# Writing phase products from SBUF into operand tiles, and weaving the first mixing visit between the phase steps

## The chip, the cores and the metric

One core of one Trainium2 chip. The metric is device time of one execution in microseconds (us). Executions of one kernel in one set spread over 0.1 to 0.6 %, so only differences whose intervals lie apart are taken as shown. A run of the kernel before always lies beside a run of a variant, on the same chip. Two variants that were not run in the same call are compared through the kernel before, and such a difference is uncertain by some 6 to 9 us where the intervals are widest (both taken together). Engines are named as the profile names them: PE (TensorE matmul), PEld (its weight load), DVE (VectorE), ACT (ScalarE), POOL (GpSimd), SP (SyncE).

## The reference, cut to what matters

```python
def reference(x, h, w_theta, w_tok_r, w_tok_i, w_ch):   # x: (8, 5696, 128), h: (5696, 128)
    y = causal_convolution_by_fft(x, h)                  # (8, 5696, 128)
    theta = y @ w_theta
    zr, zi = y * cos(theta), y * sin(theta)              # "phase products"
    mix = w_tok_r @ zr + w_tok_i @ zi                    # over 5696 tokens, for each batch: "mixing"
    u = y + mix
    return u + maximum(u @ w_ch, 0)
```

The mixing is most of the work: two 5696 x 5696 weights against 1024 columns (8 batches of 128). The kernel splits 5632 = 2 x 2816 of the tokens in both directions and forms the 2 x 2 block product with seven products instead of four (Strassen-Winograd style), which needs sums of operand blocks.

## The kernel before: the parts that the change touches

Three stages matter. The FFT leaves y (transposed) in memory and partly in SBUF. The **phase steps** turn 22 token tiles of 128, in two halves of four batches, into zr and zi. The **mixing visits** follow: the first full one of each of two passes (one for each half of the input tokens) is "classic" (four products, 176 matmuls of 512 columns), while the other full ones use seven products and the operand sums.

A phase step: four PE transposes, ten matmuls for theta, one DVE copy out of PSUM, three ACT functions, two DVE products, then stores:

```python
def phase_step(ti, hh):                       # tile ti, half hh of the batches
    ps = psum()
    ...                                       # transposes into tpz, then:
    y_ap = st["sby"].tile([P, 4, D], BF16, tag="y", name="y_ap")     # slots: 2 in half 0, 4 in half 1
    def copy():
        nc.vector.tensor_copy(y_ap, tpz)
        nc.sync.dma_start(y2_hbm[ti]..., y_ap...)                   # y is needed again later
    phases_b(ti, y_ap, ..., copy=copy)

def phases_b(...):
    ...                                       # theta matmuls
    if copy is not None: copy()
    nc.scalar.activation(mag, r, AF.Abs)
    nc.scalar.activation(red, r, AF.Sin, ...)
    nc.scalar.activation(mag, mag, AF.Sin, ...)
    zz = fh.tile(...)
    zi_eng.tensor_mul(zi, red, yflat)         # DVE
    nc.vector.tensor_mul(zr, mag, yflat)
    ...
    nc.sync.dma_start(z_hbm[:, p_, j, i, :, cols].rearrange("z t n -> t z n"), zz[rows])
```

So every product goes to memory (`z_hbm`) and comes back as one of eleven operand tiles `b` (1 MB each). The steps of both halves run first, then the visits:

```python
for n, ti in enumerate(tile_order):           # 22 steps of the second half
    phase_step(ti, 1)
    ...                                       # every fourth: load finished operand tiles
...                                           # pools of the mixing are opened only here
for i, (k, p, tt, j0, s0, nj) in enumerate(stretches):   # 3 operand tiles a stretch
    if (p, tt, j0 + s0) in ((1, None, 0), (1, 1, 0)):    # DVE in written order: start of pass 2 only
        ...
    if classic:                               # first visit of a pass
        for n in range(4):
            for j in range(nj): ... four matmuls
            aside(n == 0, n == 2)             # a "background" phase step of a later tile
        for j in range(nj):
            sums_apart(...); sums_in_place(...)   # five DVE sums for each operand tile
```

## Time and profile before

| | us |
|---|---|
| median of the runs | 2174.2 |
| first second-half copy on DVE | 477.9 |
| first mixing matmul | 549.4 |
| second visit begins | 590.8 |
| PE full from about | 596 |

I add one table: columns are the stretch and its length, then busy us (number of instructions) of PE, PEld, DVE, ACT and POOL, then PE's granted clock, the share of the DMA engines and GB/s. The kernel before, by stages:

```profile
478.00:500.00 22.00, 13.99 (x147) 10.14 (x149) 18.39 (x34) 17.80 (x32) 0.00 (x0) 0.96 0.87 224
500.00:520.00 20.00, 10.59 (x86) 8.07 (x88) 15.06 (x28) 11.63 (x21) 7.54 (x17) 0.67 1.01 255
520.00:540.00 20.00, 4.71 (x41) 3.18 (x38) 11.85 (x23) 7.75 (x14) 6.01 (x12) 0.67 1.13 291
540.00:560.00 20.00, 10.40 (x37) 4.41 (x39) 10.55 (x21) 2.74 (x5) 10.51 (x20) 0.63 1.15 287
560.00:580.00 20.00, 19.89 (x101) 9.43 (x102) 17.12 (x31) 4.33 (x7) 6.12 (x12) 1.00 1.04 266
580.00:600.00 20.00, 17.69 (x79) 7.88 (x80) 17.54 (x32) 3.73 (x6) 3.77 (x8) 0.91 0.72 158
600.00:640.00 40.00, 39.79 (x204) 19.01 (x206) 31.69 (x62) 12.38 (x20) 16.54 (x31) 1.00 0.79 153
```

Read PE downwards: 14, 11, 5, 10, then 20 of 20. From 500 to 560 no engine is full, while the DMA share is above 1.0 of its nominal: the steps and the read-back of their products wait on transfers. That hole is what the change is after.

### The profile page before, as it was taken

Reading aid. Unit: us, or ns where it says so; the run is one execution under the profiler, and the core shown is the slowest. Engines: PE = TensorE matmul, PEld = TensorE weight load, DVE = VectorE, ACT = ScalarE, POOL = GpSimd, SP = SyncE. Lnnn points to the kernel's source line nnn. Section 1 sums busy time; section 2 is a strip of 40 time slices with the busy share of each in tenths; the row PEclk is TensorE's granted clock in tenths of the full one; section 3 lists DMA queues with packets and bytes.
Section 4 is the critical chain, followed back from the end, with each engine's and each line's share of the span. In section 5 each row is a group of like instructions: output and inputs, shape, how many; then the busy total and the mean of one; then the engine's idle time right before and its main releaser. Section 6 shows DMA issues by size and latency. Waiting matters only on the chain.

```text
span 2175.5 us, 41105 instructions
## 1 busy us (share of the span) xinstructions
PE 1998.2 (92%) x15545; PEld 1125.1 (52%) x15723; DVE 1619.4 (74%) x2920; ACT 670.6 (31%) x984; POOL 857.1 (39%) x1572
## 2 busy tenths in 40 slices
PE   4788898763899999999999999899999999999998
PEld 4787888652344444444444444344444444444444
DVE  7767767767778888888877667667777777776867
ACT  5877877574132333333210000001111111111111
POOL 5301010002344645445466544354545453535350
PEclk8788889987899999999999999999999999999999
DMA  7356463579988989899999869687878787879794
GB/s 146 89 125 163 128 162 118 172 185 275 236 156 175 182 169 168 167 179 176 176 169 162 138 115 291 106 133 137 148 132 152 132 151 130 152 131 153 126 158 91
DMA packets 409382, 340.38 MB, mean 156 GB/s; under 512 B 83303, under 2 KB 363751, under 8 KB 408071
## 3 DMA queue, kind: packets, MB, share of 16 engines
q0 software_dynamic: 221312, 143.00, 48.7%
q1 hardware_dynamic: 183552, 179.93, 28.5%
q10 hardware_dynamic: 4320, 14.81, 1.8%
q8 instruction: 123, 2.02, 0.4%
q14 instruction: 75, 0.61, 0.1%
HBM read 381.83 MB, written 97.93 MB: 221 GB/s over the span
## 4 chain that ended last, share of the span: by engine, by line
PE 65%; DMA 5%; DVE 4%; issue 2%; ACT 2%; POOL 1%; SPq 1%; DVEq 0%; ACTq 0%; POOLq 0%
PE m L910 59%; DMA b<-z_hbm 3%; PE m L878 2%; DMA z_hbm<-zz 2%; DVE c L917 1%; PE v L680 1%; PE utp L673 1%; PE m L914 1%; DVE wt L591 1%; PE m L833 1%; POOL wb L582 1%; PE m L831 1%; ACT mag L404 0%; ACT red L405 0%; PE theta_ps L382 0%
## 5 line engine op out<-in xcount | busy, mean ns | idle before, releaser
L582 POOL DMA_DIRECT2D wb<-in_moe_w_tok_i_dram x720 | 387.9, 547 | 679.3 <-DVE wt L591 602.6
L591 DVE STREAM_TRANSPOSE wt<-wb 128x384 f32<-128x384 f32 (+2 forms) x720 | 360.2, 524 | 117.1 <-PE m L910 71.2
L582 POOL DMA_DIRECT2D wb<-in_moe_w_tok_r_dram x720 | 386.6, 548 | 146.2 <-DVE wt L591 107.0
L910 PE MATMUL m<-b,wt 128*128 128x512 bf16 x1803 | 425.7, 381 | 7.1 <-DVE wt L591 2.4
L910 PEld LDWEIGHTS <-wt 128*128 128x128 bf16 x1848 | 181.3, 98 | 225.0 <-issue 5.7
L917 DVE TENSOR_TENSOR c<-c,m 128x512 f32<-128x512 f32 x420 | 271.0, 671 | 0.4 <-PE m L910 0.4
L675 ACT ACTIVATE uts<-utp 128x512 bf16<-128x512 bf16 (+1 forms) x90 | 53.2, 592 | 607.3 <-PE utp L673 607.3
L320 PE MATMUL ps<-r_u,u_t 128*128 128x128 f16 x1024 | 133.0, 228 | 14.9 <-DVE u_t L304 11.7
L321 PE MATMUL ps<-r_v,v_t 128*128 128x128 f16 x1024 | 131.7, 227 | 0.0
L670 ACT ACTIVATE ub<-c 128x512 bf16<-128x512 f32 (+1 forms) x90 | 56.3, 628 | 224.9 <-DVE c L846 139.7
L127 POOL DMA_DIRECT2D x<-in_x_dram x64 | 34.2, 541 | 201.3 <-PE ps L190 189.3
L320 PEld LDWEIGHTS <-u_t 128*128 128x128 f16 x1024 | 106.0, 103 | 13.6 <-DVE u_t L304 13.5
L321 PEld LDWEIGHTS <-v_t 128*128 128x128 f16 x1024 | 104.9, 103 | 5.2 <-issue 3.7
L304 DVE TENSOR_TENSOR u_t<-xs,hs 128x1024 f16<-128x1024 f16 x96 | 69.6, 725 | 41.9 <-ACT xs L302 31.5
L302 ACT ACTIVATE xs<-ps 128x1024 f16<-128x1024 f32 x96 | 95.3, 1017 | 17.6 <-DVE v_t L304 8.7
L878 PE MATMUL m<-b,wt 128*128 128x512 bf16 x344 | 79.3, 387 | 15.3 <-ACT red L405 14.5
L190 PE MATMUL ps<-f_t,x 89*128 89x180 f16 x512 | 84.5, 310 | 8.0 <-ACT xs L302 5.9
L208 PEld LDWEIGHTS <-w_t 64*128 64x128 f16 x3240 | 65.5, 106 | 38.1 <-issue 24.7
L580 POOL COPY wb<-b 128x2 bf16<-128x2 bf16 x4 | 0.5, 179 | 213.2 <-DMA z_hbm<-zz 213.2
L190 PEld LDWEIGHTS <-x 89*128 89x128 f16 x512 | 73.8, 237 | 10.1 <-issue 9.4
L384 ACT ACTIVATE red<-theta_ps,magic 128x512 f32<-128x512 f32 (+1 forms) x46 | 31.6, 687 | 140.8 <-PE theta_ps L382 107.4
L623 ACT ACTIVATE yb<-tpz 128x512 bf16<-128x512 bf16 (+1 forms) x46 | 27.4, 597 | 153.6 <-PE tpz L621 137.4
(2713 smaller groups left out, 3824.5 us busy)
## 6 DMA issues: line engine op xcount, KB each, us to landing
wb<-in_moe_w_tok_r_dram POOLq DMA_DIRECT2D x352, 96.0 KB, 4.5
wb<-in_moe_w_tok_i_dram POOLq DMA_DIRECT2D x352, 96.0 KB, 5.0
wb<-in_moe_w_tok_r_dram POOLq DMA_DIRECT2D x352, 80.0 KB, 4.2
wb<-in_moe_w_tok_i_dram POOLq DMA_DIRECT2D x352, 80.0 KB, 3.7
hs<-hf_hbm SPq DMA_DIRECT2D x192, 128.0 KB, 3.2
cp_hbm<-c SPq DMA_DIRECT2D x88, 256.0 KB, 2.3
c<-cp_hbm SPq DMA_DIRECT2D x88, 256.0 KB, 4.0
out_dram<-c SPq DMA_DIRECT2D x88, 256.0 KB, 4.2
```

The lines of the kernel that those rows point to most:

```text
L190: nc.tensor.matmul(ps[:, i // 2, (i % 2) * 2 * K1:(i % 2 + 1) * 2 * K1], lhs(q + i), f1_t[:NB], start=True, stop=True)
L208: nc.tensor.matmul(ps[:, e, j * HD:(j + 1) * HD], w_t2[rows, c0 + j, N2 * (1 - ri):N2 * (3 - ri)], a_st["a"][rows, ri * K1 + c0 + j, :], s ...
L302: nc.scalar.activation(xs[:, :, :, :ck], ps, AF.Copy)
L304: nc.vector.tensor_tensor(uv[r][:, :, :, c0:c0 + ck], xs[:, :, :, :ck], hv[:, r:r + 1, :, :ck].to_broadcast([P, 2, HD, ck]), op=mult)
L320: nc.tensor.matmul(o, u_t[:, at:at + P], r_u, start=True, stop=False)
L321: nc.tensor.matmul(o, v_t[:, at:at + P], r_v, start=False, stop=True)
L582: nc.gpsimd.dma_start(wb[32 * i:32 * i + 32, :ng, :nj * 64], bass.AP(tensor=a.tensor, offset=a.offset + row0 * S + p * H + i * QR + j0 * 6 ...
L591: nc.vector.transpose(wt.rearrange("p j t r -> p (j t r)").bitcast(F32).rearrange("p (j g t) -> p g j t", j=TJ, g=4)[:, :ng, :nj], wb[:, : ...
L670: nc.scalar.activation(ub[:m].rearrange("p b d -> p (b d)"), c[:m], AF.Copy)
L878: nc.tensor.matmul(ms[n // 2 * 2 + h], a[n][:, j, :, r], bts[jj][n % 2 * 2 + h][:, r, :], start=(n % 2 == 0 and jj == 0 and r == 0), stop= ...
L910: nc.tensor.matmul(ms[q], a[q][:, j, :, r], bts[jj][q][:, r, :], start=(jj == 0 and r == 0), stop=(jj == NJ - 1 and r == 1 and q not in left))
L917: nc.vector.tensor_tensor(c, z, ms[q], op=op)
```

## The change

Its intent: for nine of the eleven operand tiles the second half's products go from SBUF straight into the operand tile (the first half is loaded beforehand), weights can be loaded early into the place of an FFT table, and the first visit's matmuls are woven between the last twelve phase steps. The sums of operands are spread over steps and visit, and DVE is put in written ("program") order from the first of the ten steps that precede the first visit to the third stretch of the second.

```diff
+                for r in range(2):                            # products: SBUF -> operand tile
+                    (nc.gpsimd if e and r else nc.sync).dma_start(
+                        home[j][32 * i:32 * i + 32, :4096]....[:, :, q_, r], zz[e * 64 + r:e * 64 + 64:2])
 ...
+    def load_b_half(j):                                       # first half, from memory, on POOL
+        t_ = home_of[j] = tile_b(0, j, home_pool(j))
+        for z in range(2):
+            nc.gpsimd.dma_start(t_[:, z * 2048:z * 2048 + 1024], z_hbm[z, 0, j, 0]...)
 ...
+            (nc.gpsimd if hh else nc.sync).dma_start(y2_hbm[ti]..., y_ap...)
 ...
-    for n, ti in enumerate(tile_order):
-        phase_step(ti, 1)
+    steps1 = [lambda ti=ti: phase_step(ti, 1) for ti in tile_order]
+    def next_steps(n):
+        if steps1:
+            for _ in range(n):
+                steps1.pop(0)()
+                done["steps"] += 1
+                sum_some(1)                                   # one operand sum that is due
 ...
-            if (p, tt, j0 + s0) in ((1, None, 0), (1, 1, 0)):
-                if tt is None:
+        if (p, tt, j0 + s0) in ((0, 0, 0), (0, 1, 6), (1, None, 0), (1, 1, 0)):
+            if tt != 1:
                 ordered.enter_context(tc.manual_schedule(engines={mybir.EngineType.DVE}))
 ...
+                next_steps(10)                                # ten steps ahead of the first visit
 ...
                 for j in range(nj):
                     ...four matmuls
+                    if p == 0:
+                        if steps1:
+                            next_steps(1)                     # twelve steps woven into its first stretch
+                        else:
+                            sum_some(1)
```

What `manual_schedule` does can be read from the traces: inside it DVE's instructions stand as they are written; outside it the build puts them in an order of its own.

## The prediction

> **What bounds the kernel now.** I read the page's engine rows first, then a table of stages, then the waits and the DVE groups inside the one stage where PE is idle. Page, busy tenths in 40 slices (54 us each):
>
> ```profile
> PE   4788898763899999999999999899999999999998
> ...
> PEclk8788889987899999999999999999999999999999
> DMA  7356463579988989899999869687878787879794
> ```
>
> PE is full from slice 12 on. The hole is in slices 9 to 11 (435 to 600 us), where the granted clock sags too while DMA is at 8 to 9 tenths. The same by stage; columns are busy us (instructions) of PE, PEld, DVE, ACT, POOL, then clock, DMA share, GB/s:
>
> ```profile
> 440.00:478.00 38.00, 24.92 (x323) 19.63 (x330) 21.67 (x39) 26.68 (x45) 0.00 (x0) 0.84 0.77 190
> 478.00:550.00 72.00, 29.88 (x272) 21.75 (x277) 53.92 (x99) 39.92 (x69) 19.59 (x40) 0.74 1.01 260
> 550.00:595.60 45.60, 42.99 (x201) 19.72 (x205) 34.37 (x62) 8.07 (x13) 13.28 (x25) 0.95 0.94 229
> 595.60:1286.00 690.40, 684.01 (x3393) 322.21 (x3462) 554.79 (x1082) 170.50 (x275) 358.58 (x660) 1.00 0.93 166
> 1286.00:1420.00 134.00, 124.75 (x563) 56.92 (x570) 87.45 (x170) 4.80 (x9) 57.05 (x107) 0.96 0.82 185
> 1420.00:2160.00 740.00, 735.89 (x3839) 354.09 (x3915) 546.01 (x1064) 97.16 (x162) 342.19 (x638) 1.00 0.79 139
> ```
>
> From 595.6 on PE is 99% busy, so each us by which that steady state starts earlier is a us off the end. Two stages lie ahead of it and run one after the other: the 22 phase steps on batches 4 to 7 (478 to 550), then the first ("classic") mixing visit with its 176 matmuls (550 to 595.6). Neither fills an engine: in 117.6 us PE is busy 72.9, DVE 88.3, ACT 48.0. Why the first takes 72 us, from the waits in 478 to 550:
>
> ```profile
> POOL wb L580 <- DMA z_hbm<-zz: 213.2, 1, 213.2
> ACT mag L404 <- DVE y_ap L486: 32.1, 13, 9.8
> PE ps L482 <- ACT red L405: 26.9, 14, 10.2
> ...
> PE m L878 <- ACT red L405: 14.5, 1, 14.5
> PEld L878 <- DVE y_ap L486: 13.5, 1, 13.5
> DVE b L543 <- DMA b<-z_hbm: 11.3, 6, 4.6
> ```
>
> The mixing matmul m stands behind the last phase step; the weight loads stand behind phase products that go to memory (z_hbm) and come back; DVE, in order, stands behind the read-back of b, and the phase steps behind DVE. DVE groups of 478 to 596 (count, then busy us and mean ns):
>
> ```profile
> L415 DVE TENSOR_TENSOR zz<-mag,y_ap 128x512 bf16<-128x512 f32 x24 | 16.5, 686 | 0.0
> ...
> L486 DVE COPY y_ap<-ps 128x512 bf16<-128x512 bf16 x22 | 9.2, 419 | 2.4 <-DMA y_hbm<-y_ap 1.9 <-PE ps L399 0.4
> L591 DVE STREAM_TRANSPOSE wt<-wb 128x384 f32<-128x384 f32 x17 | 8.7, 553 | 4.0 <-DMA wb<-in_moe_w_tok_i_dram 4.0
> L543 DVE TENSOR_TENSOR b<-b 128x1024 bf16<-128x1024 bf16 x11 | 7.6, 688 | 16.2 <-DMA b<-z_hbm 16.2
> ```
>
> In the timeline these overlap by some 0.08 us: start to start 0.60 for a product or an operand sum, 0.34 for a copy, 0.50 for a transpose. I use those.
>
> **What the Trainium skill says.** (1) "Perfetto Trace Analysis", section Optimization Strategy: where the busiest engine changes between regimes, interleaving the regimes can help. That is this change, and the table above is the case: ACT and DVE lead in the first stage, PE in the second. (2) "TensorE: Matmul & The Clock Gate", section What's actually happening: PE falls to half clock after about 3.4 us without work and needs about as long to recover. The trace agrees: clock 0.50 in 540 to 550, 0.77 in 550 to 560, 1.00 in 560 to 590, and the steps' wide matmuls start 0.43 us apart after a gap, 0.22 otherwise. (3) "VectorE: DVE Perf Modes", section The perf-mode tier table: a tensor_tensor on bf16 in SBUF reaches 2x and no more, so spreading the 55 sums does not make one cheaper; 1024 columns in 0.60 us at 0.96 GHz is 1.8 a cycle. (4) "DMA: Bandwidth & Descriptors", section Issuing engines are not separate DMA queues: transfers from SP, ACT and POOL share the same 16 engines. So moving stores to POOL buys only issue time; the trace is at a DMA share of 1.01 here.
>
> **The change part by part.** It doesn't change the arithmetic; it moves it.
>
> Products: for 9 of 11 operand tiles the second half of z goes straight from SBUF into the tile. Read-back falls from 9 x 1 MB to 9 x 0.5 MB, so 4.7 MB less of the 21.6 MB moved in 478 to 560: at 263 GB/s 18 us of DMA time, mostly not on the path as such, but it removes DVE's 16.2 us wait for the read-back. Cost: 4 DMAs of 64 KB per step instead of 2 of 128 KB, one on POOL.
>
> Weights: the ring lies where an FFT table was, so its first loads leave when the last FFT stage lets go (about 405 us), no longer behind z. The 213 us POOL wait goes; it cost only the 4 us that a transpose waited.
>
> Weaving, with DVE kept in program order. Ten steps come first; each then stands behind 4 mixing matmuls.
> - Ten steps: DVE 10 x (0.34 + 2 x 0.60) = 15.4, and about 4 sums that are ready, 2.4: 17.8 us. ACT (1.66 a step in the trace): 16.6. DVE sets it.
> - Two sets of weight transposes, 8 x 0.50: 4.0.
> - Twelve woven steps: DVE 12 x (1.54 + 0.60 for a sum) = 25.7; PE 12 x (1.1 + 4 x 0.216) = 23.6; ACT 20. DVE again.
> - The other 128 matmuls: PE 27.6 + 1 for two background steps. DVE 32 sums 19.2, 8 transposes 3.5, two background steps 3.6, four adds 2.4, the next visit's weights 4.4: 33.1. DVE again; some 7 of 55 sums are left for the next visit, whose DVE is 80% busy and takes them.
> Sum 80.6 us, against the 117.6 of now. From 478 the steady state would start at 558.6: 37 us earlier, 38 with the 1.2 us of half clock just after 595.6. So the stage stays bound by DVE and not by PE (63 us).
>
> Then I take off, as estimates: 2.5 us for a later start, since the read-back of the first halves (9 x 0.5 MB) now falls into 440 to 478, where DMA stood at 254 GB/s and share 0.99 in 460 to 470; and 6 us of DVE waits on transfers, because POOL now issues 16 weight loads of 0.547 us (8.8 us) right when the woven steps need it for their y and z pieces, while y has four buffers (about 6.5 us). That leaves 29.5.
>
> Second pass: its classic visit finishes two of four sums earlier, and the in-place operand sums leave the tail (now 5.2 us from 1406.1 to 1411.4): 2 to 3 us gained. Against it, b is read back in 2 KB rather than 4 KB pieces where PE already waits 4.0 us for it: 1 to 2 us lost. Net +1.
>
> 2174.2 - 29.5 - 1 = 2143.7; I say 2145.
>
> **The rivals.**
> - Clean overlap: transfers never stall DVE and the start does not slip. 38 to 40 us gained: 2134 to 2136. More needs a start before 478. For: a DMA share with 18 us less in it. Against: steps now wait up to 10 us on stores, and their number grows.
> - Queues fill: z pieces land as late as now (up to 11.5 us at the worst), DVE in program order waits at a sum, and POOL's loads hold up stores. 15 to 20 us lost again: 2155 to 2165. For: z_hbm stores land after 5.6 us (median) in this stage, a sum is let in two steps (3.4 to 4.3 us) after its last product.
> - Lockstep: today ACT's first operation of a step starts just after that step's copy (the 32.1 us row). If that is a true dependence and DVE stays in program order, the next copy follows this step's products, which follow ACT: about 1.7 + 0.7 + 0.6 + 0.5 = 3.5 us a step, 22 x 3.5 = 77 us for what I count as 43.5. That eats the gain: about 2175. Against: theta and the transposed y now lie in different PSUM tiles, so ACT need not wait for the copy.
>
> **Range and chances.** The first rival bounds it below, the second above; half the lockstep would give 2160. So 2130 to 2165. Faster by over 2% means under 2130.7, 43.5 us off, which is more than DVE's work allows from a start at 478: 0.13. Slower by over 2% (over 2217.7) needs a stall in every later visit: 0.03. Within 2%: 0.84.
>
> **What would show it.** Right: the steady state starts near 566; DVE over 90% busy from the first second-half step to it, PE near 70% at clock 1.00; no DVE wait on the read-back of b; PE after it unchanged at 99%. Wrong: a period near 3.5 us between ACT's Abs operations (lockstep); DVE sums waiting on zz transfers or copies on y stores for over 10 us (queues); the first half of the steps ending well before or after 478; or PE below 98% in the later visits through late weight loads.

## The result, and the profile after

The kernel after took 2178.7 us (median of 4 runs, 2173.95 to 2179.79), the kernel before 2173.25 us (2172.23 to 2176.88) beside it. The ratio is 1.0018 with a 95 % interval of 0.9998 to 1.0037. All ratios here are the mean time of one kernel's runs over the mean of the other's of the same rounds, so not quite the ratio of the medians quoted. Executions over 1.5% slower than the fastest of the same kernel are left out of the means. The predicted 29.5 us did not come. The profiled execution of after is its fastest one (2173.95), and that of before is one of its slower ones (2177.26): in the two profiles after is 3.3 us the shorter, though its median is the longer. So a lead of some 3 us that is left at a point of these two profiles is no gain.

The kernel after, the same stages as above:

```profile
478.00:500.00 22.00, 12.09 (x108) 8.77 (x109) 13.99 (x26) 15.54 (x27) 11.01 (x20) 0.72 0.94 311
500.00:520.00 20.00, 16.55 (x138) 10.06 (x139) 19.37 (x37) 12.55 (x23) 10.41 (x19) 1.00 0.64 137
520.00:540.00 20.00, 19.20 (x134) 10.54 (x134) 12.22 (x23) 9.99 (x18) 11.26 (x21) 1.00 0.79 188
540.00:560.00 20.00, 13.90 (x63) 6.18 (x62) 14.04 (x25) 5.27 (x9) 2.15 (x4) 0.83 0.81 230
560.00:580.00 20.00, 9.26 (x51) 4.51 (x49) 18.30 (x33) 6.42 (x11) 8.64 (x16) 0.90 0.81 147
580.00:600.00 20.00, 16.89 (x70) 7.47 (x73) 13.42 (x27) 0.00 (x0) 8.54 (x16) 0.85 0.66 119
600.00:640.00 40.00, 34.62 (x165) 15.55 (x166) 32.71 (x65) 12.84 (x21) 13.83 (x26) 0.96 0.72 138
```

The hole from 500 to 540 is filled (PE 36 of 40 instead of 15), and the first mixing matmul comes at 508.3 instead of 549.4. But a new hole lies at 540 to 600: PE 40 of 60, where before had 48 of 60, and even 600 to 640 isn't full. The 41 us of lead shrink to 7.8 when the second visit begins (583.0 against 590.8), and to 2.6 at its last add (632.84 against 635.45), which is no more than the two profiled executions differ by. The DMA share is below 0.85 from 500 on, so the DMA engines as a whole are no longer full; single stores are still waited for, as shown below.

DVE isn't full in that hole either, and its timeline shows why (columns: start, duration, engine, line, operation, tiles, forms, count, and in brackets the idle time just before and what ended it). The kernel after, DVE, from the last step on:

```profile
545.59 0.68 DVE L622 TENSOR_TENSOR b<-b 128x1024 bf16<-128x1024 bf16 x1
546.19 1.95 DVE L686 STREAM_TRANSPOSE wt<-ring 128x384 f32<-128x384 f32 x4
...
549.24 4.30 DVE L622 TENSOR_TENSOR b<-b 128x1024 bf16<-128x1024 bf16 x7
558.11 0.69 DVE L389 SCALAR_TENSOR_TENSOR red<-red,mag 128x512 f32<-128x512 f32 x1 [4.58 <-ACT mag L388]
560.25 0.69 DVE L417 TENSOR_TENSOR red<-red,ring 128x512 bf16<-128x512 f32 x1 [1.45 <-ACT red L408]
...
564.62 5.47 DVE L622 TENSOR_TENSOR b<-b 128x1024 bf16<-128x1024 bf16 x9
...
578.77 2.49 DVE L622 TENSOR_TENSOR b<-b 128x1024 bf16<-128x1024 bf16 x4
581.18 1.28 DVE L972 TENSOR_TENSOR c<-yy,m 128x512 f32<-128x512 bf16 x2
582.38 1.49 DVE L686 STREAM_TRANSPOSE wt<-ring 128x384 f32<-128x384 f32 x3
```

and PE in the same time, at the two places where it waits for those transposes:

```profile
546.82 3.17 PE L957 MATMUL m<-b,wt 128*128 128x512 bf16 x7 [5.88 <-DVE wt L686]
...
583.01 1.04 PE L1002 MATMUL m<-ring,wt 128*128 128x512 bf16 x2 [4.53 <-DVE wt L686]
```

DVE stood still 4.58 us for ACT while 23 sums (L622) stood behind it, and it came to the second visit's weight transposes only at 582.38, behind all of them. PE then had nothing to do. Whether the sums could have run earlier, this trace alone doesn't say; e1 does. The page "PSUM — Partial Sum Buffer" of the Trainium skill, section Engine vs sequencer instructions, says that these engines' queues are strictly first in, first out. This trace agrees: nothing overtook the instruction that waited 4.58 us.

Two earlier losses are in the steps. DVE's waits between 462 and 600 (total us, times, longest):

```profile
DVE y_ap L560 <- DMA y_hbm<-y_ap: 22.7, 4, 8.8
DVE red L389 <- ACT mag L388: 4.6, 1, 4.6
```

and POOL, which now issues half loads, weight loads and y stores:

```profile
472.67 4.75 POOL L617 DMA_DIRECT2D b<-z_hbm  x9 [39.30 <-DMA y_hbm<-y_ap]
...
512.98 2.20 POOL L488 DMA_DIRECT2D ring<-in_moe_w_tok_r_dram  x4 [5.32 <-DVE zz L418]
515.18 2.15 POOL L488 DMA_DIRECT2D ring<-in_moe_w_tok_i_dram  x4
```

The half loads stood 39.3 us for an earlier transfer, and then nine were issued in 4.75 us, while DVE waited for y stores; the first second-half copy slipped from 477.9 to 484.85. The second block of weight loads (16 in all, 513 to 523) went ahead of y stores, and a copy of DVE waited 7.23 us for a y slot until 527.61.

### The profile page after: what moved, and what is told of

It reads as the page before. It is cut to its first block, busy times and chain, and to the rows that moved or that the text cites. A ratio compares the mean times of both kernels' runs of the same rounds, so it can differ in the third digit from the quotient of the medians.

```text
span 2172.2 us, 41203 instructions
## 1 busy us (share of the span) xinstructions
PE 1996.8 (92%) x15546; PEld 1123.2 (52%) x15723; DVE 1617.8 (74%) x2920; ACT 670.0 (31%) x984; POOL 888.5 (41%) x1626
## 4 chain that ended last, share of the span: by engine, by line
PE 62%; DMA 4%; DVE 3%; issue 2%; POOL 1%; ACT 0%; DVEq 0%; ACTq 0%; POOLq 0%; SPq 0%
PE m L1002 56%; PE m L957 2%; DVE c L1009 2%; DMA b<-z_hbm 2%; POOL ring L488 1%; PE v L773 1%; PE utp L766 1%; DMA ring<-in_moe_w_tok_r_dram 1%; PE m L1006 1%; DVE wt L686 1%; PE m L911 0%; DMA ring<-in_moe_w_tok_i_dram 0%; PE m L909 0%; PE theta_ps L385 0%; PE tpz L714 0%
## 5 line engine op out<-in xcount | busy, mean ns | idle before, releaser
L488 POOL DMA_DIRECT2D ring<-in_moe_w_tok_i_dram x720 | 387.5, 545 | 701.6 <-DVE wt L686 618.6
L488 POOL DMA_DIRECT2D ring<-in_moe_w_tok_r_dram x720 | 386.3, 546 | 233.6 <-PE ps L211 104.1
L686 DVE STREAM_TRANSPOSE wt<-ring 128x384 f32<-128x384 f32 (+2 forms) x720 | 358.8, 524 | 102.7 <-PE m L1002 71.9
L1002 PE MATMUL m<-b,wt 128*128 128x512 bf16 x1644 | 396.8, 381 | 3.7 <-DVE wt L686 1.5
L768 ACT ACTIVATE ring<-utp 128x512 bf16<-128x512 bf16 (+1 forms) x86 | 50.9, 592 | 608.6 <-PE utp L766 608.6
L957 PE MATMUL m<-b,wt 128*128 128x512 bf16 x314 | 74.6, 387 | 6.5 <-DVE wt L686 5.9
L716 ACT ACTIVATE ring<-tpz 128x512 bf16<-128x512 bf16 (+1 forms) x46 | 27.5, 597 | 140.5 <-PE tpz L714 111.8
L775 DVE SCALAR_TENSOR_TENSOR c<-v,c 128x512 f32<-128x512 f32 (+1 forms) x90 | 61.3, 683 | 11.7 <-PE v L773 11.6
```

Source lines behind the costliest of these rows:

```text
L488: nc.gpsimd.dma_start(wb[32 * i:32 * i + 32, :ng, :nj * 64], bass.AP(tensor=a.tensor, offset=a.offset + row0 * S + p * H + i * QR + j0 * 6 ...
L686: nc.vector.transpose(wt.rearrange("p j t r -> p (j t r)").bitcast(F32).rearrange("p (j g t) -> p g j t", j=TJ, g=4)[:, :ng, :nj], wb[:, : ...
L775: nc.vector.scalar_tensor_tensor(c[:m], v[:m], 0.0, c[:m], op0=ALU.max, op1=ALU.add)
L957: nc.tensor.matmul(ms[n // 2 * 2 + h], a[n][:, j, :, r], bts[jj][n % 2 * 2 + h][:, r, :], start=(n % 2 == 0 and jj == 0 and r == 0), stop= ...
L1002: nc.tensor.matmul(ms[q], a[q][:, j, :, r], bts[jj][q][:, r, :], start=(jj == 0 and r == 0), stop=(jj == NJ - 1 and r == 1 and q not in left))
```

## The experiments

Theory: program order is the cause. DVE's total of work would fit, but in written order it waits at the head of its line for ACT or a store while work that could run stands behind. Rivals: POOL's queue delays the stores; the background phase steps are too coarse; the weave itself is bad; the direct writes are worth nothing. Medians and ratios are against the kernel before, and a gain in us is (1 - ratio) times 2177.

| run | median us | ratio | 95 % interval |
|---|---|---|---|
| change as built | 2178.7 | 1.0018 | 0.9998 to 1.0037 |
| e1 free order | 2150.16 | 0.9874 | 0.9852 to 0.9896 |
| e2 y stores on SP | 2183.39 | 1.0023 | 1.0000 to 1.0045 |
| e3 background steps split | 2175.08 | 0.9986 | 0.9968 to 1.0005 |
| e4 steps first, in order | 2167.79 | 0.9955 | 0.9935 to 0.9976 |
| e5 free, steps first | 2149.14 | 0.9872 | 0.9839 to 0.9904 |
| e6 free, half loads spread | 2149.95 | 0.9876 | 0.9845 to 0.9907 |
| e7 order in visit 1 only | 2176.56 | 0.9995 | 0.9966 to 1.0024 |
| e8 free, through memory | 2157.24 | 0.9909 | 0.9882 to 0.9937 |
| e9 order in the steps only | 2160.01 | 0.9925 | 0.9901 to 0.9948 |
| e10 order in the tail only | 2167.83 | 0.9963 | 0.9938 to 0.9989 |
| e11 free, four y slots | 2142.95 | 0.9841 | 0.9815 to 0.9867 |
| e12 before, four y slots | 2172.4 | 0.9972 | 0.9957 to 0.9987 |
| e13 as built, four y slots | 2171.67 | 0.9970 | 0.9953 to 0.9986 |
| e14 free, four slots, steps first | 2146.23 | 0.9854 | 0.9831 to 0.9876 |

All gave correct results.

### e1: the change without program order in the first pass

```diff
-        if (p, tt, j0 + s0) in ((0, 0, 0), (0, 1, 6), (1, None, 0), (1, 1, 0)):
-            if tt != 1:
+        if (p, tt, j0 + s0) in ((1, None, 0), (1, 1, 0)):
+            if tt is None:
```

> The changed kernel with DVE's program-order region taken away from the first visit (kept in the second pass as it was). Theory A (order: DVE, held in program order, stands at round trips of others, in the changed kernel 18 us idle between 485 and 583 us: 7.2 and 2.3 us on y stores, 4.6 + 1.5 + 1.5 us on the background steps, the rest at the end): the free order lets other work pass and the kernel gets 8 to 15 us faster than the changed one, some 2163 to 2170. Theory B (work: DVE is simply full there): within 3 us of the changed kernel. Theory C (transfers: y stores and operand loads land late whatever the order): within 3 us too, with the waits moved to other instructions. If the free order puts operand sums ahead of products that others wait for, it may even be slower; then A has no support from here.

Measured: 2150.16 us, ratio 0.9874, 27 us better than before and 31 us better than the change as built, where theory A had expected 8 to 15: right in kind, too small in size. Same stages:

```profile
478.00:500.00 22.00, 9.36 (x59) 6.64 (x60) 12.14 (x22) 9.34 (x17) 11.21 (x21) 0.59 1.03 320
500.00:520.00 20.00, 18.28 (x170) 11.38 (x169) 18.77 (x37) 17.79 (x32) 14.49 (x27) 1.00 0.89 212
520.00:540.00 20.00, 19.93 (x158) 11.54 (x157) 20.00 (x39) 15.45 (x28) 9.39 (x18) 1.00 0.74 208
540.00:560.00 20.00, 17.69 (x89) 8.21 (x88) 19.85 (x35) 2.17 (x5) 7.27 (x14) 1.00 0.87 218
560.00:580.00 20.00, 18.02 (x97) 8.50 (x96) 16.59 (x31) 8.33 (x14) 10.21 (x19) 1.00 1.08 219
580.00:600.00 20.00, 19.03 (x99) 8.92 (x97) 16.27 (x33) 9.44 (x15) 8.58 (x16) 1.00 1.01 171
600.00:640.00 40.00, 40.00 (x205) 18.85 (x203) 34.80 (x68) 11.21 (x18) 17.15 (x32) 1.00 0.90 178
```

DVE is full (39.85 of 40) from 520 to 560, and the second visit begins at 565.4. That is close to the 566 at which the prediction had its steady state, but in part by luck: the first second-half copy comes at 494.47 here and not at 480.5, DVE then needs 70.9 us to the second visit and not 86.6, and PE is full only from 600 (37.05 of 40 in 560 to 600). The same instructions as above, in the order that the build chose; DVE of this run:

```profile
546.89 0.64 DVE L622 TENSOR_TENSOR b<-b 128x1024 bf16<-128x1024 bf16 x1
547.46 1.08 DVE L686 STREAM_TRANSPOSE wt<-ring 128x256 f32<-128x256 f32 x3
548.47 10.89 DVE L622 TENSOR_TENSOR b<-b 128x1024 bf16<-128x1024 bf16 x18
559.28 0.57 DVE L686 STREAM_TRANSPOSE wt<-ring 128x384 f32<-128x384 f32 x1
560.89 0.69 DVE L389 SCALAR_TENSOR_TENSOR red<-red,mag 128x512 f32<-128x512 f32 x1 [1.03 <-ACT mag L388]
```

Eighteen sums run without a pause, then the second visit's transposes, 23 us earlier than in the kernel after, and the wait for ACT is 1.03 us. The program-order region is the main cause. One thing moved with it: POOL's queue, too, came out in another order. In e1 eight weight loads are issued at 472 to 477, ahead of the half loads, and the 16 loads that stood in one block at 513 to 523 lie singly among the y stores. How much of the 31 us is DVE's own line and how much POOL's is not taken apart here; e9 and e10 bound it.

### e2: y stores on SP instead of POOL

```diff
-            (nc.gpsimd if hh else nc.sync).dma_start(y2_hbm[ti]...
+            nc.sync.dma_start(y2_hbm[ti]...
```

> The changed kernel with one word altered: the y stores of the second-half phase steps go out from SP again, not from POOL behind the weight loads. If POOL's queue is what holds the y stores (the 7.2 us stall at 520 us follows 16 weight loads issued from 513.0 to 522.9), that stall and the 2.3 us one vanish and the stage ends 6 to 9 us earlier; SP then issues 4 transfers a step at 0.6 us, 2.4 us against a step's 2.3, so up to 2 us may come back. Net 4 to 9 us faster than the changed kernel. If the stores are late because the 16 engines are full (theory C), nothing changes, under 2 us.

Measured: 2183.39 us, ratio 1.0023: nothing gained. The waits on y stores behind the weight loads did go: the 11.6 us that are left (8.46 at 482.34, 3.15 at 490.11) belong to first-half copies, whose stores were on SP before too. But with SP issuing y and z pieces both, the products now waited for slots of zz or with no releaser shown (6.14 us at 537.88), and from the first second-half copy to the last step's end it took 62.9 us (493.00 to 555.95) against 61.3 in the kernel after. So the wait moved from y to zz, and the second visit began at 596.3. POOL's queue alone is not the cause.

### e3: background steps in three parts with sums between

```diff
             nc.scalar.activation(mag, theta_ps, AF.Copy)
+            yield                             # DVE parts of a background step are emitted apart
             nc.vector.scalar_tensor_tensor(red, red, MAGIC, mag,
...
         nc.scalar.activation(mag, mag, AF.Sin, ...)
+        yield
...
-                aside(n == 0, n == 2)
+                aside(n == 0, {1: "a", 2: "b", 3: "last"}.get(n, False))     # (first pass)
```

> The changed kernel with each background phase step of the program-ordered stretch cut in three, with operand sums between the parts, so that DVE meets each part after ACT has done with the one before. Same instructions. Theory A: DVE's waits of 4.6, 1.5 and 1.5 us on ACT between 553 and 572 us go away, and some 3 us of PE stalls in the next visit: 5 to 9 us faster than the changed kernel. Theory B: these waits only shift, since DVE's work must be done before the next visit's weights: under 2 us.

Measured: 2175.08 us, ratio 0.9986, no difference from before within the interval. Against the change as built it is 7 us better by the ratios and 3.6 us by the medians, in different calls, so it doesn't settle whether 5 to 9 us or under 2 were gained. The wait for ACT at L389's place stayed 4.1 us, and the waits on y stores stayed at 22.1. Splitting by hand did not take the head of the line away.

### e4: all 22 steps first, in program order

```diff
-                next_steps(10)
+                next_steps(22)
```

> The changed kernel with all 22 second-half steps ahead of the first mixing visit: nothing woven, products still straight into the operand tiles, sums still spread. If DVE sets the pace of this stage (as the prediction has it), weaving PE's 48 matmuls between steps buys little: within 5 us of the changed kernel, with PE idle in the steps and DVE as full as before. It would even lose POOL's weight loads from the middle of the steps, which cost 7 us. If weaving is what pays (PE's matmuls hidden under the steps), it is 10 to 20 us slower than the changed kernel.

Measured: 2167.79 us, ratio 0.9955, so 14 us better than the woven change as built (1.0018). Its first mixing matmul comes at 540.2, 32 us later, and still the second visit begins at 582.6, as in the kernel after (583.0), after which PE is fuller. So in program order the woven kernel is the slower one. That need not be the weave alone: with the steps first, POOL's weight loads no longer stand in their middle, as the expectation says, and DVE's waits on y stores fell from 22.7 to 16.1 us. The two are not separated.

### e5: free order, steps first

Both edits, e1 and e4.

> The release from program order together with all 22 second-half steps ahead of the first mixing visit (no weave). If weaving is worth something once VectorE is free to take its work in the order of readiness, this is slower than the free weave of the earlier run (2150 us): by 5 to 12 us, so 2155 to 2162. If VectorE alone sets the end of this stretch (it is over 90 % busy from the first step to the second visit), the order of TensorE's work is worth nothing and the time is 2148 to 2152.

Measured: 2149.14 us, ratio 0.9872 against 0.9874 for the woven version. Once DVE is free, writing the weave by hand is worth nothing that these intervals (some 5 us either way) can show. But this kernel is not unwoven on the chip: the build's own order starts the first visit's matmuls at 494.1, earlier than in e1 (499.2), and sets them one by one between the matmuls of the steps, which last until 538.6. Whether the overlap of steps and visit pays in itself is therefore not tested by this run; among these kernels only e4, in program order, lacks the overlap. That DVE's total of work sets the second visit's start fits, but is not shown by it.

### e6: free order, half loads issued one behind each step

```diff
+        def load():
             for z in range(2):
                 nc.gpsimd.dma_start(t_[:, z * 2048:z * 2048 + 1024], z_hbm[z, 0, j, 0]...)
+        late.append(load)
...
                 steps1.pop(0)()
+                if late:
+                    late.pop(0)()
```

> The release from program order, and the nine loads of half operand tiles on the GpSimd queue issued one behind each second-half step instead of nine at once. Theory that the late start (VectorE idle 9.5 us at 474 to 483 on the store of y) comes of these nine loads standing ahead of the y stores: the idle stretch falls below 3 us and the time to 2142 to 2146. Rival, that the loads only move their wait behind the first matmuls (or that the store is late for the memory traffic itself): 2148 to 2153, and the first mixing matmul no earlier than 497 us.

Measured: 2149.95 us, ratio 0.9876: a miss. The idle stretch is still there (9.56 us, until 478.67), because POOL doesn't keep the written order either: six half-load transfers still went together at 476.9. The copy that waits there is one of the *first* half, whose y has two slots. This run doesn't test the spreading, but it pointed to e11.

### e7: program order for the first visit only

```diff
-        if (p, tt, j0 + s0) in ((0, 0, 0), (0, 1, 6), ...
+        if (p, tt, j0 + s0) in ((0, 0, 0), (0, 1, 0), ...      # released at the second visit
```

> Program order of VectorE kept over the first visit with its woven steps, but released from the start of the second visit on (as built it lasts to the second visit's last stretch but one). If the loss sits in the woven steps and the first visit's tail, this is 2170 to 2179, near the change as built; if it sits in the second visit (late transposes behind sums there), it comes down to 2150 to 2158. I expect 2168.

Measured: 2176.56 us, ratio 0.9995. Nearly the whole loss is still there, so it sits in the first visit and its steps, not in the second visit.

### e8: free order, second-half products through memory

```diff
-             tags=None, copy=copy, home=home_of if hh else {})
+             tags=None, copy=copy, home={})
...
+                for j, t_ in home_of.items():
+                    if last_of[j] == done["steps"]:            # last step that writes tile j
+                        for z in range(2):
+                            nc.sync.dma_start(t_[:, z * 2048 + 1024:z * 2048 + 2048], z_hbm[z, 0, j, 1]...)
```

> The release from program order, but the second half's products through memory again: stored to the z tensor and the half tiles loaded back, one load behind the last step that writes a tile. If the direct write from SBUF to SBUF is what makes the early first visit possible, the first matmul comes 4 to 8 us later than 499 and the time is 2155 to 2162. If the weave and the order of VectorE do it all and a round trip through memory is hidden behind the ten steps' work, 2148 to 2153.

Measured: 2157.24 us, ratio 0.9909, which is 7.6 us slower than e1 (0.0035 times 2177; different calls, and the intervals just overlap). PE's first mixing matmuls of this run, and of e1:

```profile
L963 PE MATMUL m<-ring,wt x15: 376/379/631, 503.5 to 537.8; 128*128 128x512 bf16 x15
```

```profile
L957 PE MATMUL m<-ring,wt x16: 379/379/457, 499.2 to 526.2; 128*128 128x512 bf16 x16
```

They start 4.3 us later and end 11.6 us later. The 4.3 us at the start are not the direct write's: the first second-half copy is already as late (498.85 against 494.47), before any product of that half is made. From there the lag grows to 9.2 us at the second visit (574.6 against 565.4). So the direct write seems to be worth some 5 us by the profiles and 7.6 by the ratios, a minor part of e1's 27, and with the overlap of the intervals it is not shown beyond doubt. The rest lies with the early half loads, early weights and spread sums, which I did not take apart.

### e9 and e10: the program order cut in two

e9 keeps it for the 22 steps and the first stretch (12 woven steps included), e10 from the second stretch to the third stretch of the second visit:

```diff
-        if (p, tt, j0 + s0) in ((0, 0, 0), (0, 1, 6), ...
+        if (p, tt, j0 + s0) in ((0, 0, 0), (0, 0, TJ), ...      # e9
+        if (p, tt, j0 + s0) in ((0, 0, TJ), (0, 1, 6), ...      # e10
```

> VectorE in program order only while the 22 second-half steps and the first stretch of the first visit are emitted; free from the second stretch on. Theory that the loss of program order has two parts, the stall of the steps on stores of y behind the weight loads (7 us at 528 in the change as built) and the tail of the visit, where transposes of weights, sums and waiting steps of phases stand in one line (some 20 us): this run keeps the first part only, 2156 to 2163. Rival, that all is lost in the steps: 2172 to 2178.

> The complement: VectorE free while the steps and the first stretch are emitted, in program order from the second stretch of the first visit to the second visit. The same theory: keeps the loss of the tail, 2166 to 2174. Rival, that all is lost in the steps: 2148 to 2153.

Measured: e9 2160.01 us (0.9925), e10 2167.83 us (0.9963). Against e1's 0.9874 that is a loss of 11 us for the order in the steps and of 19 us for the order in the tail. Together 30 us, and the order as a whole costs 31 (1.0018 less 0.9874). The two parts add up within their intervals (each difference is uncertain by some 7 us), so a third cause of a few us isn't excluded. POOL's 16 weight loads stand in one block again in e9 (from 518.85), as in the kernel after, and not in e10, where they lie among the y stores as in e1. So what POOL's order costs is a part of the 11 us, while the 19 us come without that block. In e10 the head of the line is plain, DVE first and then PE in the same time:

```profile
540.40 2.49 DVE L622 TENSOR_TENSOR b<-b 128x1024 bf16<-128x1024 bf16 x4
553.23 0.69 DVE L389 SCALAR_TENSOR_TENSOR red<-red,mag 128x512 f32<-128x512 f32 x1 [10.34 <-ACT mag L388]
```

```profile
535.83 11.39 PE L957 MATMUL m<-b,wt 128*128 128x512 bf16 x51
547.05 0.39 PE L714 MATMUL tpz<-ident_bf,yT 128*128 128x128 bf16 x4
547.28 4.48 PE L957 MATMUL m<-b,wt 128*128 128x512 bf16 x19
551.59 0.39 PE L385 MATMUL theta_ps<-w_theta_sb,yT 128*128 128x128 bf16 x4
```

DVE's next instruction is a part of a background step. Its ACT input waits for theta, which PE computes only at 551.59, in its own line behind 70 matmuls. So DVE idles 10.34 us with the sums and transposes behind it that e1 does in this time, and PE pays later: at 578.5 it waits 4.05 us for the second visit's transposes.

### e11: free order, four slots for y in the first-half steps

```diff
-        sby = pool("s2y", 2, pha, reuse_waits="tile")
+        sby = pool("s2y", 4, pha, reuse_waits="tile")
```

> The release from program order, and four slots instead of two for the y tiles of the first-half steps, so that VectorE need not wait at 474 to 483 us for a y store that lands late. If the late start is only the want of a slot, VectorE's 9.5 us idle stretch falls under 3 us and the time to 2141 to 2146. If the steps then wait for something else that is late at the same moment (operands of the second half from memory, at a transfer share above 1.0), 2147 to 2153 with the idle stretch under another name.

Measured: 2142.95 us, ratio 0.9841, the best of all: 1.6 % under before. The page "Perfetto Trace Analysis" of the Trainium skill, section Optimization Strategy, says that gaps that repeat can mean that SBUF or PSUM for the next tile is lacking. Here it was one gap of 9.5 us and not a repeating one, and a slot was indeed what it lacked. The gain on e1, 0.9874 to 0.9841, is 7 us, but across calls and with intervals that just overlap; e12 tests the slots directly. DVE's waits of this run between 462 and 600:

```profile
DVE zz L417 <- DMA z_hbm<-zz: 9.4, 3, 4.6
DVE b L622 <- DMA b<-z_hbm: 4.7, 2, 3.9
DVE y_ap L560 <- DMA y_hbm<-y_ap: 1.8, 2, 1.3
```

The wait on y fell from 10.2 us in e1 to 1.8. Much of it came back under other names: waits for slots of zz are 9.4 us now, and those on loads of b 4.7 instead of 3.0. From 462 to the second visit DVE idles 17.9 us in both kernels; what e11 has is 4 us less work left at 462 (81.27 us busy instead of 85.46). The first mixing matmul comes at 489.6 (e1: 499.2) and the second visit at 561.1 (e1: 565.4).

### e12, e13, e14: whose gain are the slots?

The same one-line edit in the kernel before (e12), in the change as built (e13), and with e1 and e4 together (e14).

> The kernel before, with nothing but four slots instead of two for the y tiles of the first-half steps. It too has VectorE idle 5 us at 473 on a y store, but its first mixing matmul waits for transfers until 549 us at a transfer share above 1.0. If those transfers set its start, the slots are worth less than 2 us: 2174 to 2179, ratio 0.998 to 1.000. If VectorE's line sets it, 2168 to 2173. I expect 2177.

> The change as built, program order and all, with four slots instead of two for the y tiles of the first-half steps. If the late start and the loss to program order simply add, the slots are worth 5 to 7 us here as in the free order: 2170 to 2174. If the line in program order waits further on for the same late thing (transposes of weights, phases), less than 3 us: 2176 to 2180. I expect 2173.

> Free order, four y slots, and all 22 second-half steps ahead of the first mixing visit instead of woven into it. With two slots the weave was worth nothing (2149 against 2150). If VectorE's total of work sets the second visit's start, the same holds here: 2140 to 2146. If the earlier start makes TensorE's order count, it is slower than the woven 2143: 2148 to 2153.

Measured: e12 2172.4 us (0.9972), e13 2171.67 us (0.9970), e14 2146.23 us (0.9854). The slots are worth 6 us in the kernel before too, more than I expected: its first matmul moves from 549.4 to 536.2. Yet the second visit begins at 591.4 (590.8 in before), so the earlier start is lost again by then. Of the 3.5 us by which the two profiled executions differ (2173.78 against 2177.26), 2.2 lie in the second visit (last add at 633.27 against 635.45): PE waits 1.11 us for DVE there and not 2.21, and its clock in 595.6 to 600 is 1.00 and not 0.61. Where the rest lies stays open. In program order they are worth about 10 us across calls. So of e11's 35 us some 6 to 7 are to be had without the change, and some 28 are the change in free order. e14 against e11: writing the weave by hand again makes no difference that the intervals can show, with the reserve made at e5.

## Why the prediction was wrong

The bottleneck was named rightly: DVE, and the start of the steady state. One slip of bookkeeping comes first: the 117.6 us of "now" run to 595.6, where PE is full, but the sum ends where the second visit begins, which is 590.8 in the kernel before. So 4.8 us of the forecast lead were counted too much, whatever DVE does. The gain was worked out for a DVE that does its work back to back, 80.6 us with 6 us of waits on transfers. **The step that failed is the sum for "Weaving, with DVE kept in program order"**: it added durations and left out what program order makes of them. Step by step, in the kernel after:

| term of the sum | predicted us | measured us |
|---|---|---|
| later start | 2.5 | 6.9 (477.9 to 484.85; in e4, e9, e7 and e2, with the same first half, 11 to 15) |
| ten steps | 17.8 | 22.45 (to 507.3; 2.3 of it one wait on y) |
| eight transposes | 4.0 | 3.7 |
| twelve woven steps | 25.7 | 34.6 (to 545.6; 7.2 of it one wait on y) |
| the rest, to the second visit | 33.1 | 37.4 (to 583.0; 7.5 of it on ACT) |
| waits on transfers, apart | 6 | in the rows above |
| DVE in sum | 86.6 | 98.2 |

- **The rest**, the tail, is the largest term by the runs: 19 us. Its 4.3 us in the table are only the part before the second visit. The other part comes in that visit, which took 49.84 us to its last add against 44.65 (PE 34.62 of 40 in 600 to 640, where 39.79 had been). That transposes and sums follow late there is a reading: freeing the order in that visit alone (e7) gained nothing.
- **The steps** are 11 us. The wait of 7.2 us behind the 16 POOL loads was seen coming and put at 6 us with all other waits; with the 2.3 us the waits on y alone came to 9.5. That these waits make up the 11 us is argued: e9 has both DVE's order and POOL's block of weight loads, and no run parts them in free order. A smaller part was not in the sum at all: in program order the copy's own product follows it directly and starts 0.51 us after it (529.94 to 530.45), not 0.34 as in the free order of before, which is 0.17 us in each of 22 steps, 3.7 us as an estimate.
- **The late start** was 7 us or more, not 2.5. The copies that waited are first-half ones with two y slots; with four, the wait fell to 1.8 us in e11, though much of it came back on slots of zz and on loads of b.
- **The rivals.** "Lockstep" isn't seen: the period is 2.32 us a step and not 3.5. "Queues fill" came nearest: it had DVE in program order waiting at a sum, and POOL's loads holding up stores, and gave it 2155 to 2165. The stores came true, and so did its sign, copies waiting on y stores for over 10 us: 22.7 us, of which 13.1 lie before the first second-half copy. No sum waited for the read-back of b. That is the kind of e9's 11 us. The tail, where ACT and not a transfer is waited for, no rival had.
- **Signs.** Steady state at 566: no, past 583. DVE over 90 % busy: no, 61 % in 520 to 540 and 70 % in 540 to 560. PE unchanged after: yes (59.68 of 60 in 640 to 700, both kernels). In free order (e1) DVE is 95 % busy from the first second-half copy to the second visit (67.30 of 70.91 us), and that visit begins at 565.4; but PE is full only from 600, it is 93 % busy in that stretch and not 70, and DVE waits 3.0 us for loads of b. PE after it is unchanged there too (60.00 of 60).
- **The second pass** was given +1 us. I find nothing to tell it apart from the spread of the runs.

That the program-order region was the cause is shown (e1, e7, e9, e10). For the tail its mechanism is seen in the traces: DVE's line waiting for ACT, 4.58 us in the kernel after and 10.34 in e10. For the steps it is DVE's line and POOL's order together, not parted. Why the order was written in, these runs don't say.

## What to carry to other kernels

A sum of an engine's durations is a floor that holds only if something ready always stands at the head of its line; with an order fixed by hand, follow each wait of the line back, over ACT and PE, before counting on the sum. Free the order first, and look for the missing slot next: one tuple and one number turned here a change that had moved nothing into 35 us, some 6 of which the slots give without the change. And before you weave two stages by hand, look at whether the build already does it: in free order the weave as written and the steps written first took the same time, because the build overlapped them in both.

## What the Trainium skill lacked or had wrong

- "Perfetto Trace Analysis", Optimization Strategy: interleaving regimes is recommended where the busiest engine changes. It lacks the condition, and who does the interleaving. In program order the woven kernel was 14 us slower than the steps first (as built 1.0018, e4 0.9955), perhaps in part for its weight loads; in free order the build interleaves by itself, and writing it by hand gave nothing (e1 0.9874, e5 0.9872).
- "PSUM — Partial Sum Buffer", Engine vs sequencer instructions: the strict queues are stated, but not what an order is worth. Here fixing the order of one engine's queue, over the steps, the first visit and two stretches of the second, cost 31 us (other queues' order changed with it).
- "DMA: Bandwidth & Descriptors", Issuing engines are not separate DMA queues: agrees with e2, which gained nothing by moving y stores from POOL to SP. It doesn't give what a transfer of a size takes to land while others run beside it: y stores of 128 KB landed after 2.2 us (median) in the kernel before between 470 and 490, and after 4.6 us in the kernel after, where the half loads ran beside them (that they are the cause is not isolated).
- "VectorE: DVE Perf Modes", The DRAIN you can't avoid: a semaphore between two DVE instructions is said to cost nothing, from a chain of copies. In the kernel after, a copy is followed 0.51 us after its start by the product that reads its result; in the kernel before by the product of another step after 0.34 us (475.58 to 475.92). That the dependence makes the 0.17 us is argued from the code, no run isolates it.
